# A statically ordered attention and mixer kernel: shorter latencies in the order's model, and stage settings chosen anew for them

## The chip, the cores and the metric

One core of a Trainium2 chip. The metric is the device time of one execution in microseconds. Every run of a kernel was timed on the same chip as runs of the kernel before, in alternating rounds; medians are given with the lowest and highest run. The clock quoted is the mean TensorE clock that was granted in a run, as a share of full speed.

## The reference

The input `x` has 2048 rows of 512 values. A gate per row mixes two branches: attention with 32 heads of width 16, and a mixer with two layers. Everything is bfloat16.

```python
def reference(A_x, A_wqkv, A_wo, B_x, B_w1, B_w2, B_w3, B_w4, gate_w):
    def _A_ref(x, wqkv, wo):
        ...                                   # q, k, v: 32 heads of 16
        scores = jnp.einsum("bhqd,bhkd->bhqk", q, k) * (Dh ** -0.5)
        p = _softmax(scores, axis=-1)
        o = jnp.einsum("bhqk,bhkd->bhqd", p, v)
        return (...)(o, 0, 2, 1, 3).reshape(B, S, D) @ wo
    def _B_ref(x, w1, w2, w3, w4):
        h = _gelu(_layernorm(x, axis=-1) @ w1)
        ...                                   # four column groups shifted by 1 or 2 rows
        hs = jnp.concatenate([g0, g1, g2, g3], axis=-1) @ w2
        x1 = x + hs
        h2 = _gelu(_layernorm(x1, axis=-1) @ w3) @ w4
        return x1 + h2
    g = _sigmoid((x * gate_w).sum(-1, keepdims=True))
    return g * a + (1 - g) * b                # a, b: the two branches
```

The scores make 2048 tiles of 128 keys by 512 queries, and all of them have to be exponentiated. ScalarE does it with its own function, in pairs of tiles; VectorE does it for about 28% of the tiles by arithmetic on the bits of the number, with the help of shifted copies that VectorE or GpSimd makes. At the end of each round but the last (32 rounds, each of four heads and 512 queries) the sums are copied out of PSUM.

## The kernel before

The order of instructions on each engine is not written by hand. While the program is built, the kernel runs a small event model of the five engines, picks what an engine does next whenever it is free, and emits instructions in the order of the model's times. On the chip each engine works through its list strictly in that order, and semaphores hold it where a result is missing. So the model's numbers (`hold`, how long an engine is taken, and `lat`, how much later the result counts as seen) never hold anything up on the chip; they only decide the order.

```python
class Job:
    def __init__(self, eng, hold, lat, deps, fn, prio=5, acq=(), frees=(), at=0, name="", port=False): ...

class Sim:
    def emit(self, t, fn):
        if fn is not None:
            self.n += 1
            self.order.append((t, self.n, fn))

    def try_engine(self, e):
        ...                                    # the ready job of the best priority is j
        j.start = self.t
        self.emit(self.t, self.in_port_order(e, j.fn) if j.port else j.fn)
        self.t_free[e] = self.t + j.hold
        ...
        self.push(self.t + j.hold + j.lat, lambda: self.finish_job(j))   # only now do dependents become ready
```

The helpers give each engine its latency. Line 321 holds the settings by stage: 32 score tiles are a stage, and a stage may overrule any of 24 numbers of the picking rule (how far ahead scores run, when a shift goes to GpSimd, how urgent the end of one of the 32 rounds, each of four heads and 512 queries, is, and so on). They come from a search outside the kernel.

```python
    def dve(hold, deps, fn, **kw):
        return sim.add(Job("DVE", hold, 280.0, deps, fn, **kw))
    def act(hold, deps, fn, **kw):
        return sim.add(Job("ACT", hold, 160.0, deps, fn, **kw))
    def gp(hold, deps, fn, **kw):
        return sim.add(Job("POOL", hold, 250.0, deps, fn, port=True, **kw))
    def dma(lat, deps, fn, hold=450.0, **kw):
        return sim.add(Job("SP", hold, lat - hold, deps, fn, **kw))
```

At the end of each round but the last (32 rounds, each of four heads and 512 queries) the sums are copied out of PSUM, and the softmax denominators in them go through two transfers: first to a small buffer `den` in DRAM, then back, spread over 128 partitions, to `pk`. VectorE then forms reciprocals. The model takes 2.0 us for each transfer:

```python
    def finish_round(r):
        ...
        e = dve(PSUM_NS, round_ops[r], lambda: nc.vector.tensor_copy(out=ab.slot[:], in_=acc[:]), acq=[ab], prio=0)  # L1033
        d0 = dma(2000.0, [e], lambda: nc.sync.dma_start(out=db.slot[:], in_=ab.slot[0:P:32, :]), prio=1, acq=[db],
                 frees=[ab])                                                                                       # L1036
        d1 = dma(2000.0, [d0], lambda: nc.sync.dma_start(
            out=kb.slot[:], in_=db.slot[:].rearrange("j (b e) -> (j b) e", e=16)), prio=1, acq=[kb], frees=[db])   # L1038
        r1 = dve(160, [d1], lambda: nc.vector.reciprocal(out=kb.slot[:], in_=kb.slot[:]), prio=0)                  # L1040
        r2 = dve(90, [r1] + jg[1], ...)          # times the gate
        d2 = dma(2000.0, [r2], ...)              # pk to DRAM, then four broadcasts d3 to bcs
        n = gp(1250, d3, lambda: nc.gpsimd.tensor_tensor(out=ob.slot[:], in0=ab.slot[:], in1=bb.slot[:], op=ALU.mult),
               acq=[ob], frees=[ab, bb], prio=0)                                                                   # L1050
```

The second place is the normalised input of the mixer, `xn`: VectorE writes 32 tiles into two buffers in turn, and each goes to DRAM by a transfer before its buffer is free again.

```python
        for t in range(4 * c, 4 * c + 4):
            xb = Buf("xn", 1)
            g = dve(323, [m], lambda t=t, xb=xb: nc.vector.tensor_scalar(out=xb.slot[:], in0=x_sb[:, t, :], ...),
                    prio=0.35, acq=[xb], port=True)                                                                # L695
            ds.append(dma(2200.0, [g], lambda t=t, xb=xb: nc.sync.dma_start(
                out=xn_dram[which, t * P:(t + 1) * P, :], in_=xb.slot[:]), frees=[xb]))
```

The softmax here doesn't subtract the row's maximum and nothing guards it: scores larger than these inputs give would overflow.

## Time and profile before

| | before |
|---|---|
| median of the first 3 runs (lowest to highest) | 772.55 us (772.16 to 772.81) |
| span of the profiled execution, granted clock | 770.4 us, 1.000 |
| ScalarE waiting before its pairs (L922) | 16.8 us |
| VectorE waiting for score tiles in the ring (L948) | 23.6 us in 62 pieces |
| VectorE waiting for a transfer | 0.3 us (0.2 us of it in the one piece that the list below shows) |

Three engines are over 94% busy, so a microsecond in which ScalarE, VectorE or TensorE stands still between 20 and 755 us can be a loss of time. The prediction below shows the main groups and stretches. One line of the list of waits of the kernel before is needed besides. A line says who waited at which line for whom, then the total in us, how often, and the longest:

```profile
DVE pk L1040 <- DMA pk<-den: 0.2, 1, 0.2
```

The reader is to see that VectorE's reciprocals, which depend on a transfer, cost practically no waiting in this kernel.

### The profile page before, as it was taken

How to read it: one execution, taken by the hardware profiler on the slowest of the kernel's cores; microseconds unless marked ns; L12 is line 12 of the kernel's file. 1: busy time of each engine (PE TensorE's matmuls, PEld its weight loads, DVE VectorE, ACT ScalarE, POOL GpSimd, SP SyncE). 2: the span in 40 equal slices, each digit the busy share in tenths (PEclk: the TensorE clock that was granted, in tenths of full speed). 3: DMA queues.
4: the chain of work that ended last, by engine and by line, in shares of the span. 5: the costliest groups of instructions: out<-in, count | busy, mean ns of one | idle time of the engine just before them, and what ended most of it. 6: DMA issues, size and time to landing. Idle time of an engine off the chain costs nothing.

```text
span 770.4 us, 23725 instructions
## 1 busy us (share of the span) xinstructions
PE 758.7 (98%) x9588; PEld 227.8 (30%) x9588; DVE 725.2 (94%) x1575; ACT 739.7 (96%) x767; POOL 335.2 (44%) x332
## 2 busy tenths in 40 slices
PE   9999999999999999999999999999999999999997
PEld 5333322223222222233232224222233222223222
DVE  6999999999999999998989998999999889999996
ACT  6899999999999999999989999999999999999995
POOL 2345533443344444344345553344454454454531
PEclk9999999999999999999999999999999999999999
DMA  9402133122001221141001001001100000000001
GB/s 192 142 3 35 54 98 88 47 72 89 6 19 34 61 72 46 48 125 50 17 18 33 23 20 47 23 27 27 41 19 19 23 19 22 27 20 20 13 18 38
DMA packets 67093, 34.60 MB, mean 45 GB/s; under 512 B 46748, under 2 KB 62380, under 8 KB 66984
## 3 DMA queue, kind: packets, MB, share of 16 engines
q1 hardware_dynamic: 66040, 32.56, 16.3%
q8 instruction: 75, 1.23, 0.6%
q10 hardware_dynamic: 944, 0.52, 0.2%
q14 instruction: 34, 0.28, 0.1%
HBM read 17.40 MB, written 6.81 MB: 31 GB/s over the span
## 4 chain that ended last, share of the span: by engine, by line
PE 71%; ACT 22%; DVE 4%; issue 3%; ACTq 0%; DVEq 0%
PE acc L1017 26%; PE psA L842 23%; PE ring L532 20%; ACT PA L922 16%; DVE PD L948 2%; ACT hT L766 2%; ACT hB L766 2%; DVE PD L984 1%; ACT hT L735 1%; ACT L922 1%; PE ring L842 1%; PE ring L510 0%; ACT L766 0%; PE ring L1295 0%; DVE hB L765 0%
## 5 line engine op out<-in xcount | busy, mean ns | idle before, releaser
L922 ACT ACTIVATE PA<-psA 128x1024 bf16<-128x1024 f32 x742 | 689.8, 1052 | 16.8 <-PE acc L1017 7.7
L986 POOL TENSOR_SCALAR PD<-PD 128x1024 uint16<-128x1024 uint16 x270 | 281.8, 1048 | 384.7 <-DVE PD L984 215.8
L948 DVE TENSOR_SCALAR PD<-ring 128x512 uint16<-128x512 f32 x565 | 372.9, 680 | 25.9 <-PE ring L842 23.6
L1017 PE MATMUL acc<-PD,V 128*17 128x512 bf16 x2260 | 307.3, 381 | 1.0 <-DVE accsb L1033 0.8
L842 PE MATMUL psA<-q,kT 32*128 32x512 bf16 x1483 | 285.8, 384 | 5.3 <-ACT PA L922 4.4
L1017 PE MATMUL acc<-PA,V 128*17 128x512 bf16 x1483 | 277.6, 381 | 0.0
L984 DVE TENSOR_SCALAR PD<-PD 128x1024 uint16<-128x1024 uint16 x579 | 226.2, 429 | 1.5 <-PE acc L1017 0.8
L842 PE MATMUL ring<-q,kT 32*128 32x512 bf16 x565 | 190.7, 384 | 0.0
L842 PEld LDWEIGHTS <-kT 32*128 32x128 bf16 x2048 | 76.8, 91 | 311.0 <-issue 309.0
L1017 PEld LDWEIGHTS <-V 128*17 128x17 bf16 x3743 | 74.9, 88 | 129.1 <-issue 107.0
L532 PE MATMUL ring<-xnT,w 128*32 128x512 bf16 x1152 | 89.0, 382 | 0.0
L532 PE MATMUL ring<-w,hT 128*32 128x512 bf16 x704 | 58.5, 383 | 0.1
L532 PEld LDWEIGHTS <-w 128*32 128x32 bf16 x1920 | 45.2, 95 | 43.9 <-issue 30.3
L1050 POOL TENSOR_TENSOR oT<-accsb,bcs 128x512 bf16<-128x512 f32 x31 | 39.5, 1275 | 24.7 <-DVE PD L984 19.4
L532 PE MATMUL ring<-w,w 128*32 128x256 bf16 (+1 forms) x768 | 41.1, 311 | 0.0
L532 PE MATMUL ring<-w,hB 128*32 128x512 bf16 x448 | 36.0, 383 | 0.0
L1033 DVE COPY accsb<-acc 128x512 f32<-128x512 f32 x31 | 21.1, 681 | 1.1 <-PE acc L1017 1.0
L675 DVE BATCH_NORM_STATS2 st<-x_sb 128x6 f32<-128x512 bf16 x32 | 21.5, 678 | 0.0
L532 PE MATMUL ring<-w,wq 128*32 128x512 bf16 x256 | 21.2, 383 | 0.2 <-ACT w L561 0.2
L532 PEld LDWEIGHTS <-hT 128*32 128x32 bf16 x704 | 14.8, 95 | 20.3 <-issue 15.5
L765 DVE CAST hT<-ring 128x512 bf16<-128x512 f32 x28 | 18.8, 680 | 1.1 <-PE ring L532 0.9
L765 DVE CAST hB<-ring 128x512 bf16<-128x512 f32 x28 | 19.0, 682 | 0.9 <-PE ring L532 0.7
(93 smaller groups left out, 263.5 us busy)
## 6 DMA issues: line engine op xcount, KB each, us to landing
bcs<-rr SPq DMA_DIRECT2D x124, 64.0 KB
xn_dram<-xn SPq DMA_DIRECT2D x32, 128.0 KB
w<-in_B_w_dram SPq DMA_DIRECT2D x5, 512.0 KB
oD<-oT SPq DMA_DIRECT2D x124, 16.0 KB
w<-in_B_w_dram SPq DMA_DIRECT2D x4, 448.0 KB
out_dram<-ot SPq DMA_DIRECT2D x14, 128.0 KB
x_sb<-in_A_x_dram SPq DMA_DIRECT2D x3, 512.0 KB
w<-in_A_wqkv_dram SPq DMA_DIRECT2D x2, 256.0 KB
```

The source lines that it names most:

```text
L532: units.append([Op("col", j, lambda j=j, lf=lf, rf=rf, n0=n0, n1=n1, st=st, sp=sp: nc.tensor.matmul(get()[32 * j:32 * j + 32, n0:n1], lhsT ...
L675: a = dve(600, deps, lambda: nc.vector.bn_stats(out=sb.slot[:], in_=x_sb[:, t, :]), prio=6, at=at, acq=[sb])
L765: pre.append(evac(g, PSUM_NS, lambda ps, m=m: nc.vector.tensor_copy(out=h2()[:, m, :], in_=ps[:])))
L766: ge = act(93 + 427 * FT + 2600, pre, lambda: nc.scalar.activation(out=h2(), in_=h2(), func=ACT.Gelu_apprx_tanh), prio=0)
L842: o = Op("row", i, lambda: nc.tensor.matmul(dst(), lhsT=kT[G][32 * i:32 * i + 32, kt * P:(kt + 1) * P], rhs=qbuf[G, c].slot[32 * i:32 * i ...
L922: job = act(hold, ops, lambda: nc.scalar.activation(out=pb.slot[:, 0:n], in_=buf.slot[:, 0:n], func=ACT.Exp, scale=0.25), acq=[pb], frees= ...
L948: nc.vector.tensor_scalar(out=pr["buf"].slot[:, h * 512:(h + 1) * 512], in0=buf.slot[:], scalar1=BITS_MUL, scalar2=BITS_ADD, op0=ALU.mult, ...
L984: return nc.vector.tensor_scalar(out=d[k][:, 0:w], in0=d[0][:, 0:w], scalar1=float(SHIFT * k), scalar2=None, op0=ALU.add)
L986: return nc.gpsimd.tensor_scalar(out=d[k][:, 0:w], in0=d[0 if both else 2][:, 0:w], scalar1=1.0, scalar2=float(SHIFT * (k if both else 1)) ...
L1017: o = Op("col", i, lambda: nc.tensor.matmul(acc[32 * i:32 * i + DH + 1, :], lhsT=lhs(), rhs=rhs(), start=st, stop=True, tile_position=(0, ...
L1033: e = dve(PSUM_NS, round_ops[r], lambda: nc.vector.tensor_copy(out=ab.slot[:], in_=acc[:]), acq=[ab], prio=0)
L1050: n = gp(1250, d3, lambda: nc.gpsimd.tensor_tensor(out=ob.slot[:], in0=ab.slot[:], in1=bb.slot[:], op=ALU.mult), acq=[ob], frees=[ab, bb], ...
```

## The change

The model's latencies for VectorE and GpSimd results are cut until the model's time from the start of an instruction to that of its dependant is close to the measured one (the prediction below works it out: 0.03 us above it), and the settings by stage are chosen anew under the shorter latencies. The idea: a model without slack can place dependants right behind their results, and packs the order tighter.

```diff
-    STAGES = {0: {'AHEAD': 6, 'EARLY': 13, 'DVE_ALONE': 150, 'S_PRIO': 0.368}, 1: {'AHEAD': 8, 'S_PRIO': 0.415}, ... }   # cut
+    STAGES = {0: {'GP2': 0.1, 'DUE_SH': -20}, 1: {'SL': (165, 180), 'PRESS': 30}, ... }                                 # cut
     def dve(hold, deps, fn, **kw):
-        return sim.add(Job("DVE", hold, 280.0, deps, fn, **kw))
+        return sim.add(Job("DVE", hold, 150.0, deps, fn, **kw))
     def gp(hold, deps, fn, **kw):
-        return sim.add(Job("POOL", hold, 250.0, deps, fn, port=True, **kw))
+        return sim.add(Job("POOL", hold, 110.0, deps, fn, port=True, **kw))
     def evac(g, hold, fn, prio=2, eng="DVE", **kw):
-        job = Job(eng, hold, 280.0, ...)
+        job = Job(eng, hold, 150.0, ...)
```

More of the change, by code (lines that the diff above doesn't have):

```diff
@@ L320 @@
     SEG = 32
-    STAGES = {0: {'AHEAD': 6, 'EARLY': 13, 'DVE_ALONE': 150, 'S_PRIO': 0.368}, 1: {'AHEAD': 8, 'S_PRIO': 0.415}, 2: {'ROT': 3, 'URG': 3, 'MAXU': 9, 'PD_LOW': 3}, 3: {'PA_LOW': 3, 'DVE_WAIT': 4}, 4: {'SL': (25, 60), 'URG': 2, 'DVE_STOP_L': 9, 'DUE_SH': 40}, 5: {'SL': (25, 60), 'URG': 2, 'DVE_STOP_L': 9, 'DUE_SH': 40}, 6: {'S_PRIO': 0.234}, 7: {'PRESS': 17, 'DVE_WAIT': 5}, 8: {'PV_FULL': 0.776, 'AHEAD': 7, 'PD_LOW': 0}, 9: {'PV_FULL': 0.877, 'ROT': 2, 'AHEAD': 6, 'PA_LOW': 0}, 10: {'PV_FULL': 0.794, 'PA_LOW': 0, 'SL': (165, 60), 'DVE_ALONE': 2}, 11: {'SL': (85, 100), 'EARLY': 62}, 12: {'EARLY': 124, 'PV_IDLE': 0.433, 'DVE_STOP_L': 11, 'SL': (25, 40)}, 13: {'GP3': 0.6, 'DVE_ALONE': 150}, 14: {'ROT': 3, 'GP3': 0.9, 'URG_L': 16, 'AHEAD2': 12}, 15: {'P1_PRIO': 0.309, 'DVE_STOP_L': 5, 'AT_SH': 60, 'DVE_STOP': 5}, 16: {'DVE_WAIT': 2, 'AHEAD2': 10}, 17: {'ROT': 1, 'AT_SH': 10, 'GP3': 0.8, 'DVE_ALONE': 2}, 18: {'P1_PRIO': 0.403, 'GP2': 0.2}, 19: {'PRESS': 10}, 20: {'URG': 7, 'AT_SH': 60, 'GP2': 0.2}, 21: {'IDLE_NS': 352, 'DVE_ALONE': 300}, 22: {'S_PRIO': 0.257}, 23: {'PRESS': 52, 'AT_SH': 60}, 24: {'PA_LOW': 3, 'PRESS': 23, 'GP3': 0.8}, 25: {'PV_IDLE': 0.414, 'AT_SH': 10}, 26: {'DUE_SH': 8, 'PD_LOW': 1, 'GP2': 0.2, 'GP3': 0.9}, 28: {'AHEAD2': 10, 'EARLY': 142}, 29: {'AHEAD': 8, 'S_PRIO': 0.388, 'GP3': 0.9, 'ROT': 1}, 30: {'PV_IDLE': 0.372, 'DUE_SH': -40, 'S_PRIO': 0.412, 'PA_LOW': 2}, 31: {'IDLE_NS': 311, 'GP3': 0.9, 'P1_PRIO': 0.22}, 32: {'DUE_SH': 40, 'DVE_STOP': 5}, 33: {'DVE_STOP_L': 7, 'SL': (205, 60)}, 34: {'P1_PRIO': 0.326, 'PD_LOW': 0, 'PV_IDLE': 0.37, 'GP2': 0.35}, 36: {'PD_LOW': 1, 'DVE_STOP': 7}, 37: {'URG': 4, 'IDLE_NS': 589}, 38: {'ROT': 2}, 39: {'EARLY': 155, 'PA_LOW': 3}, 40: {'DUE_SH': -20, 'PRESS': 8}, 41: {'P1_PRIO': 0.584, 'PA_LOW': 3, 'MAXU': 10}, 42: {'AHEAD2': 8, 'PRESS': 58, 'DVE_ALONE': 0}, 43: {'PD_LOW': 0, 'DVE_WAIT': 2, 'P1_PRIO': 0.216, 'PV_FULL': 1}, 44: {'MAXU': 7, 'ROT': 1}, 45: {'PRESS': 10, 'SL': (65, 80)}, 46: {'DVE_WAIT': 6, 'AT_SH': 120, 'PD_LOW': 0}, 47: {'DUE_SH': 80, 'P1_PRIO': 0.59, 'DVE_ALONE': 150, 'AHEAD2': 6}, 48: {'URG': 8, 'AT_SH': 120}, 49: {'PD_LOW': 3, 'ROT': 3, 'DVE_WAIT': 6, 'AT_SH': 120}, 50: {'DVE_WAIT': 1, 'SL': (5, 60), 'GP2': 0.35, 'DVE_STOP_L': 11}, 51: {'PA_LOW': 3, 'URG_L': 18}, 52: {'ROT': 2, 'PD_LOW': 1, 'PRESS': 35}, 53: {'URG_L': 16, 'IDLE_NS': 245, 'PRESS': 19}, 54: {'PD_LOW': 3}, 56: {'MAXU': 10, 'GP2': 0.1}, 57: {'URG': 2}, 58: {'ROT': 3, 'DVE_WAIT': 5}, 59: {'ROT': 1}, 60: {'GP2': 0.2, 'PV_FULL': 0.879, 'SL': (85, 100)}, 61: {'GP3': 0.6, 'GP2': 0.35, 'PV_FULL': 0.985}, 62: {'GP3': 0.6, 'GP2': 0.35, 'PV_FULL': 0.985}}
@@ new lines @@
+    STAGES = {0: {'GP2': 0.1, 'DUE_SH': -20}, 1: {'SL': (165, 180), 'PRESS': 30}, 2: {'ROT': 2, 'AT_SH': 120, 'PD_LOW': 0}, 3: {'PA_LOW': 1}, 4: {'S_PRIO': 0.598, 'GP3': 0.9, 'MAXU': 7, 'DVE_STOP': 9}, 5: {'IDLE_NS': 854, 'DVE_STOP_L': 9, 'SL': (85, 100)}, 6: {'SL': (125, 60), 'AHEAD2': 7}, 7: {'S_PRIO': 0.268, 'DVE_STOP': 8, 'PV_FULL': 0.864, 'URG': 2}, 8: {'ROT': 3, 'DVE_STOP': 7}, 9: {'PA_LOW': 1}, 10: {'GP2': 0.2, 'SL': (165, 60), 'AHEAD': 6}, 11: {'PV_FULL': 0.7, 'AHEAD2': 12}, 12: {'SL': (5, 20), 'DVE_STOP': 7, 'PA_LOW': 3, 'GP2': 0.35}, 13: {'AHEAD': 10, 'GP3': 0.8}, 14: {'P1_PRIO': 0.411, 'DVE_WAIT': 1, 'SL': (65, 60), 'PV_FULL': 1}, 15: {'DUE_SH': 8, 'DVE_STOP': 9, 'PA_LOW': 2, 'PD_LOW': 0}, 16: {'EARLY': 159, 'PV_IDLE': 0.105}, 17: {'PV_IDLE': 0.545, 'EARLY': 9}, 18: {'AHEAD2': 10, 'GP3': 0.8, 'AT_SH': 10, 'DUE_SH': -20}, 19: {'PA_LOW': 1, 'URG': 4}, 20: {'PRESS': 50, 'PD_LOW': 2, 'SL': (165, 180), 'DVE_STOP': 7}, 21: {'URG': 2, 'SL': (125, 60)}, 22: {'S_PRIO': 0.506, 'ROT': 1}, 23: {'GP3': 0.6, 'DUE_SH': 8}, 24: {'AT_SH': 30, 'GP2': 0.1, 'MAXU': 4, 'PV_IDLE': 0.35}, 25: {'GP2': 0.2}, 26: {'PRESS': 50, 'DVE_ALONE': 500, 'AT_SH': 60, 'SL': (205, 60)}, 27: {'SL': (25, 40)}, 28: {'GP2': 0.1, 'URG': 4}, 29: {'URG': 3, 'MAXU': 8, 'AT_SH': 120}, 30: {'MAXU': 11, 'PA_LOW': 0, 'DVE_ALONE': 500}, 31: {'PA_LOW': 1, 'MAXU': 7, 'GP3': 0.8}, 32: {'SL': (85, 60), 'GP2': 0.35, 'ROT': 2, 'DUE_SH': -8}, 33: {'S_PRIO': 0.295, 'SL': (165, 60), 'AHEAD': 8, 'DUE_SH': -40}, 34: {'DVE_ALONE': 500, 'DVE_STOP_L': 5, 'AHEAD2': 11, 'DVE_STOP': 5}, 35: {'PV_FULL': 0.684, 'URG_L': 19, 'PA_LOW': 2, 'PD_LOW': 0}, 36: {'DVE_ALONE': 0, 'AT_SH': 60}, 37: {'ROT': 2, 'PD_LOW': 0, 'DVE_WAIT': 2}, 38: {'EARLY': 138}, 39: {'URG': 3, 'DUE_SH': -8, 'DVE_ALONE': 2, 'PA_LOW': 3}, 40: {'PA_LOW': 3}, 41: {'DVE_STOP': 4, 'GP3': 0.8}, 42: {'ROT': 3}, 43: {'DUE_SH': 20, 'DVE_STOP_L': 10, 'DVE_STOP': 4, 'GP2': 0.35}, 44: {'URG': 4, 'ROT': 2}, 46: {'MAXU': 7, 'URG_L': 18, 'PV_IDLE': 0.292, 'GP2': 0.35}, 47: {'AT_SH': 60, 'PA_LOW': 3, 'EARLY': 115, 'IDLE_NS': 616}, 48: {'S_PRIO': 0.557, 'GP2': 0.1, 'DVE_STOP': 8, 'PV_FULL': 0.713}, 51: {'SL': (25, 60), 'AHEAD': 11, 'PV_IDLE': 0.46, 'S_PRIO': 0.395}, 53: {'AHEAD2': 7, 'GP3': 0.6}, 54: {'ROT': 3}, 55: {'DVE_STOP': 5, 'EARLY': 142, 'PRESS': 53}, 56: {'ROT': 2, 'EARLY': 154, 'PRESS': 37, 'IDLE_NS': 353}, 57: {'ROT': 1}, 58: {'DVE_STOP': 3, 'IDLE_NS': 321, 'DVE_ALONE': 300}, 59: {'ROT': 1, 'GP3': 0.9}, 60: {'PRESS': 14, 'GP2': 0.1, 'DVE_STOP': 4, 'URG_L': 15}, 61: {'PA_LOW': 1, 'DVE_ALONE': 300, 'P1_PRIO': 0.512, 'DVE_STOP': 9}, 62: {'SL': (5, 20)}, 64: {'DVE_ALONE': 2, 'SL': (25, 40)}}
@@ L541, in evac @@
     def evac(g, hold, fn, prio=2, eng="DVE", **kw):
-        job = Job(eng, hold, 280.0, [g.units[-1][-1]] if not COL else g.units[-1], lambda: fn(g.buf.slot), prio=prio,
+        job = Job(eng, hold, 150.0, [g.units[-1][-1]] if not COL else g.units[-1], lambda: fn(g.buf.slot), prio=prio,
                   frees=[g.buf] + kw.pop("frees", []), **kw)
```

## The prediction

> **What bounds the kernel now.** I read the granted clock first (1.000 on the one core, so nothing is throttled), then the page's busy shares, the groups by shape, the waits, and a table of stretches. The page's first part:
>
> ```profile
> span 770.4 us, 23725 instructions
> PE 758.7 (98%) x9588; PEld 227.8 (30%) x9588; DVE 725.2 (94%) x1575; ACT 739.7 (96%) x767; POOL 335.2 (44%) x332
> ```
>
> Three engines are nearly full at once. The work on them is fixed by how the 2048 score tiles are split: ScalarE exponentiates two tiles per instruction (L922), VectorE makes a tile by arithmetic on bits (L948) and two or three shifted copies per pair (L984), and TensorE then multiplies one matrix with V per ScalarE tile but four per VectorE tile. The groups by shape:
>
> ```profile
> L922 ACT ACTIVATE PA<-psA 128x1024 bf16<-128x1024 f32 x741 | 689.3, 1053 | 16.8 <-PE acc L1017 7.7 <-PE psA L842 4.9 <-PE ring L842 2.5
> L948 DVE TENSOR_SCALAR PD<-ring 128x512 uint16<-128x512 f32 x565 | 372.9, 680 | 25.9 <-PE ring L842 23.6 <-PE acc L1017 0.5 <-PE psA L842 0.4
> L1017 PE MATMUL acc<-PD,V 128*17 128x512 bf16 x2260 | 307.3, 381 | 1.0 <-DVE accsb L1033 0.8
> L986 POOL TENSOR_SCALAR PD<-PD 128x1024 uint16<-128x1024 uint16 x270 | 281.8, 1048 | 384.7 <-DVE PD L984 215.8 <-PE ring L842 43.7 <-PE acc L1017 39.2
> ```
>
> To see: ScalarE waits only 16.8 us before its 741 pairs; VectorE waits 23.6 us, in 62 pieces by the list of waits, for score tiles in the PSUM ring; TensorE waits for almost nobody; GpSimd has half its time free. The stretches (columns: PE, PEld, DVE, ACT, POOL busy):
>
> ```profile
> 0.00:20.00 20.00, 18.56 (x285) 10.21 (x286) 12.86 (x30) 12.66 (x17) 5.97 (x16) 1.00 0.99 188
> 20.00:380.00 360.00, 357.15 (x4485) 106.38 (x4481) 353.00 (x800) 354.73 (x371) 153.12 (x150) 1.00 0.22 59
> 380.00:420.00 40.00, 39.96 (x535) 11.44 (x530) 36.50 (x76) 36.35 (x40) 17.01 (x17) 1.00 0.08 24
> 420.00:755.00 335.00, 331.76 (x4175) 96.28 (x4171) 314.20 (x654) 328.33 (x334) 157.80 (x149) 1.00 0.09 24
> 755.00:771.00 16.00, 11.23 (x126) 3.45 (x124) 8.69 (x21) 7.65 (x10) 1.32 (x2) 0.98 0.12 38
> ```
>
> To see: between 20 and 755 us ScalarE is idle for 735 - (354.73 + 36.35 + 328.33) = 15.6 us. The other half of its idle time is start-up (7.3 us before 20) and tail (8.3 us after 755). An order of instructions can win back mainly the 15.6 us.
>
> **How tight the latencies are.** The kernel holds an event model of the five engines; run while the program is built, it decides the order of every engine's instructions, with the settings by stage. On the chip only semaphores hold things. The change concerns how long the model thinks a result takes to be seen after an instruction's slot. The timeline at a round's end, and at a shift that waits for its own tile:
>
> ```profile
> 436.05 0.67 DVE L1033 COPY accsb<-acc 128x512 f32<-128x512 f32 x1
> ...
> 436.77 0.39 PE L1017 MATMUL acc<-PD,V 128*17 128x512 bf16 x2 [0.23 <-DVE accsb L1033]
> ```
> ```profile
> 333.23 0.68 DVE L948 TENSOR_SCALAR PD<-ring 128x512 uint16<-128x512 f32 x1
> 333.95 0.85 DVE L984 TENSOR_SCALAR PD<-PD 128x1024 uint16<-128x1024 uint16 x1
> ```
> ```profile
> 433.82 1.05 POOL L986 TENSOR_SCALAR PD<-PD 128x1024 uint16<-128x1024 uint16 x1 [1.11 <-PE acc L1017]
> ...
> 434.92 0.39 PE L1017 MATMUL acc<-PD,V 128*17 128x512 bf16 x2
> ```
>
> To see: start to dependent start is 0.72 us for each of the two VectorE cases and 1.10 us for GpSimd. The model has a slot of 0.598 or 0.600 us plus 0.28, so 0.88 us, for the first two, and 1.018 + 0.25 = 1.27 us for GpSimd. So the model before is late by some 0.16 us everywhere. With the new constants it says 0.75 and 1.13 us: still 0.03 us above the chip.
>
> **What the Trainium skill says.** "Perfetto Trace Analysis", section "Per-instruction lifecycle", says that a Vector or Scalar instruction's reported end is the write's acknowledgement with the semaphore push, and that the propagation comes after it, unreported. The trace agrees: 0.05 us lie between the copy's end and the matmul. The same page, "Identifying the Most-Contended Engine", warns that matmul busy share does not measure TensorE's headroom; so I do not take the 98% for a limit by itself. "TensorEngine Tiling (Array Packing)", "Key Properties", says that changing the tiling mode drains TensorE. The chain of work shows it: a score turn of two or three matmuls takes 0.32 us though one 512-column step takes 0.22 (a 12-matmul column turn takes 0.76 us, an 8-matmul one 0.54; the difference is one step). "TensorE: Matmul & The Clock Gate", "Architectural detail", says that Vector and Scalar queues are strictly first in, first out; so a wrongly placed instruction holds all behind it. This trace does not contradict that: the stalls above have work queued behind them.
>
> **The change part by part.** I built both programs and compared their instructions; no time was taken from that. The dataflow is the same, and the counts hardly move:
> - ScalarE pairs: 741 plus one half become 740 whole. The half took 0.65 us, of which some 0.49 is slot; a pair costs 0.92 (0.904 to 0.92 start to start). Minus 1.4 us of ScalarE.
> - VectorE tiles 565 to 568, at 0.60 us: plus 1.8 us; shifts 576 + 3 halves to 575, at 0.34 us: minus 1.1 us (halves taken as 0.25 us). Plus 0.7 us of VectorE. GpSimd shifts 270 to 277, at 1.02 us: plus 7 us, beside 384.7 us of waiting, so free.
> - TensorE: score turns 742 to 739, column steps 1963 to 1960. Three turns at 0.32 + 0.11 us (the second is what an 8-matmul column turn takes above two steps) and three steps at 0.22: minus 1.9 us. Fillers 112 to 108, inside that.
> - Depth: the median number of matmuls between a score matmul and the product that uses it goes from 54 to 55 by ScalarE, and from 54 to 52 by VectorE. At 9588/742, some 13 matmuls a turn, results wait four turns, about 4 us. A 0.13 us shorter latency is small against that, and most of it is hidden.
> - Where it is not hidden: ring slots. The model sees a slot free 0.13 us sooner. Between a read's end and the next write the trace shows a median of 0.57 us. If each of the 62 ring waits shrinks by 0.13, VectorE gains 8.1 us; it makes 28% of the tiles, and I let a third reach the end: minus 2.7 us. At 31 round ends the next round's products are admitted 0.13 us sooner, 4.0 us; other column work mostly fills that, so a third: minus 1.3 us.
> - The new settings themselves: a search under a truer model should close part of the 15.6 us. I choose a fifth: minus 3 us. This is the softest term.
> - Against it: with 0.03 us of slack a late result stalls TensorE in order. I put plus 1.5 us. The tail has a whole last pair for a half: plus 0.4 us.
> - Less work on the shared bound: minus 1 us.
> The sum: -2.7 - 1.3 - 3 + 1.5 + 0.4 - 1 = -6.1 us, so 766.5 us.
>
> **Rivals.** First, TensorE stalls take the slack's place: the order is packed to 0.03 us, so every jitter of a VectorE or GpSimd result shows as a wait of products (L1017) for L948, L984 or L986. It would cost 3 to 10 us and bring 775 or more. For it: all engines are above 94%, so a stall is not absorbed. Against it: the depth of four turns, and constants that still lie above the measured latencies. Second, nothing happens: 0.13 us is lost in queues of 4 us, counts are the same, and the span stays at 770 to 773. For it: waits for products of a full PA pool (7.7 us of the 16.8) have nothing to do with these latencies. Third, the new settings pack much better, and most of the 15.6 us goes: 758 to 760. Against it: VectorE and TensorE would have to hold the same pace, and they have only 45 and 12 us unbusy, start and tail included.
>
> **Range and chances.** Faster by over 2% means below 757.1 us: 15.4 us, as good as all of ScalarE's idle time between start-up and tail. I give it 0.07. Slower by over 2% means above 788.0, which would double that idle time; 0.03. The range 759.5 to 774 leaves room for the third rival at one end and a mild first at the other.
>
> **What would show it.** Right: ScalarE's waits at L922 fall from 16.8 to about 11 us; VectorE's ring waits fall from 23.6 us towards 16; TensorE still waits for nearly nobody; durations of single instructions are unchanged. Wrong: products (L1017) waiting for VectorE or GpSimd by several us (first rival); waits unchanged in sum and only moved to other stages (second); ScalarE idle between 20 and 755 us below 6 us (third). The prediction would also be wrong if start-up or tail, which I hold fixed within 1 us, moved by several.

## The result, and the profile after

The changed kernel took 773.71 us (772.89 to 775.82, 4 runs), the kernel before on the same chip 772.36 us. The ratio is 1.0022, with a 95% interval of 1.0001 to 1.0042. So nothing was gained; the forecast was a gain of 6 us. The profiled execution spans 771.7 us at a mean clock of 0.998.

The first part of the page of the changed kernel, and its groups by shape (busy us, mean ns of one, then idle time before them and what ended it):

```profile
span 771.7 us, 23735 instructions
PE 757.2 (98%) x9593; PEld 225.2 (29%) x9593; DVE 727.1 (94%) x1574; ACT 740.6 (96%) x765; POOL 341.4 (44%) x339
```
```profile
L922 ACT ACTIVATE PA<-psA 128x1024 bf16<-128x1024 f32 x740 | 690.8, 1045 | 17.8 <-PE acc L1017 5.9 <-PE psA L842 5.6 <-PE ring L842 5.0
L948 DVE TENSOR_SCALAR PD<-ring 128x512 uint16<-128x512 f32 x568 | 375.3, 683 | 18.5 <-PE ring L842 15.9 <-PE acc L1017 0.3 <-PE psA L842 0.2
L1017 PE MATMUL acc<-PD,V 128*17 128x512 bf16 x2272 | 301.6, 382 | 2.6 <-DVE PD L984 1.8 <-POOL PD L986 0.5 <-DVE accsb L1033 0.2
...
L695 DVE TENSOR_SCALAR xn<-x_sb,rs,nm 128x512 bf16<-128x512 bf16 x32 | 11.7, 407 | 2.1 <-DMA xn_dram<-xn 2.1
L1040 DVE RECIPROCAL pk<-pk 128x16 f32<-128x16 f32 x31 | 7.6, 245 | 5.0 <-DMA pk<-den 5.0
```

The ring waits did fall as forecast, from 23.6 to 15.9 us, and single instructions last as long as before. But ScalarE waits 17.8 us instead of less, and two lines have waits of a new kind: VectorE stands 5.0 us at reciprocals and 2.1 us at `xn` tiles, for transfers. The list of waits says in how many pieces:

```profile
DVE pk L1040 <- DMA pk<-den: 5.0, 5, 1.9
...
DVE xn L695 <- DMA xn_dram<-xn: 2.1, 3, 0.8
```

The longest is at 182.6 us. The timeline there (start, duration, engine, line, operation; in brackets the idle time before and what ended it):

```profile
182.64 0.25 DVE L1040 RECIPROCAL pk<-pk 128x16 f32<-128x16 f32 x1 [1.85 <-DMA pk<-den]
182.81 0.36 DVE L984 TENSOR_SCALAR PD<-PD 128x1024 uint16<-128x1024 uint16 x1
...
183.23 0.39 PE L1017 MATMUL acc<-PD,V 128*17 128x512 bf16 x2 [1.22 <-DVE PD L984]
...
184.49 1.02 ACT L922 ACTIVATE PA<-psA 128x1024 bf16<-128x1024 f32 x1 [1.12 <-PE psA L842]
...
185.16 0.61 PE L842 MATMUL psA<-q,kT 32*128 32x512 bf16 x2
```

These lines show the mechanism. VectorE has reached the reciprocal and stands 1.85 us, because its operand is still in transit. The shift L984 is next in its list and has its data, but must wait behind. TensorE needs that shift for a product and stands 1.22 us; ScalarE needs scores that TensorE would have made in that time and stands 1.12 us. One late transfer of 8 KB has stopped all three full engines. The last line shows a second effect: a matmul of 512 columns takes 0.61 us instead of the 0.39 of the matmul at 183.23 us.

The stretches around it (us, busy time of PE, PEld, DVE, ACT, POOL, granted clock, DMA share, GB/s):

```profile
176.00:180.00 4.00, 3.84 (x49) 1.12 (x48) 3.05 (x6) 4.00 (x6) 1.55 (x2) 1.00 0.77 291
180.00:185.00 5.00, 3.59 (x34) 0.95 (x33) 2.95 (x8) 3.88 (x5) 1.04 (x1) 1.00 0.04 5
185.00:189.00 4.00, 4.00 (x27) 0.64 (x25) 2.98 (x7) 2.72 (x4) 1.04 (x1) 0.57 0.20 66
```

The denominators' first transfer was issued at 176.5 us, while four weight loads of 448 KB filled 77% of the transfer engines, and the second could only be issued 4.42 us later; the usual distance of the two issues in this trace is 1.72 us. The packet records of the trace say where that time went: the last of its four packets moved at 180.0 us, 3.5 us after the issue (usually 1.35), when the last packet of the weight loads had just ended (179.8 us). After the stall the clock of TensorE was halved for 3.4 us (0.57 in the last row), in which ScalarE worked 2.72 of 4 us.

**How far the chip lags behind its plan.** The kernel's own model can serve as a ruler. It has a planned start for every ScalarE pair; the trace has the actual start. Their difference, the drift, shows where the chip falls behind the plan. The plan's end is a number of the program's build, not a chip time; it is used only together with the drift. Over all kernels, the span is the plan's end plus the final drift plus about 8.4 us (7.5 to 8.5; mostly the tail after the model's last matmul).

| kernel | plan's end | final drift | profiled span |
|---|---|---|---|
| before | 764.6 | -2.6 | 770.4 |
| changed | 759.4 | +3.8 | 771.7 |

The new settings are worth 5.2 us in the plan. The kernel before was 2.6 us ahead of its plan at the end, since its latencies were pessimistic; the changed kernel fell 3.8 us behind. Its drift is nearly flat but for a rise of 2.9 us (from -0.7 to +2.2) between 183 and 197 us and steps of 0.75 us at 365.8, 0.73 at 636.0 and 0.66 us at 728.5. Three of these four come right after VectorE's waits for denominators: 1.85 us at 182.6, 1.25 at 632.6 and 1.14 us at 726.9. The step at 365.8 us comes 12 us after the nearest such wait, 0.63 us for an `xn` buffer at 353.8, so its cause is less plain.

### The profile page after: what moved, and what is told of

Its sections match the earlier page's. It is cut to its first block, busy times and chain, and to the rows that moved or that the text cites. A ratio compares the mean times of both kernels' runs of the same rounds, so it can differ in the third digit from the quotient of the medians.

```text
span 771.7 us, 23735 instructions
## 1 busy us (share of the span) xinstructions
PE 757.2 (98%) x9593; PEld 225.2 (29%) x9593; DVE 727.1 (94%) x1574; ACT 740.6 (96%) x765; POOL 341.4 (44%) x339
## 4 chain that ended last, share of the span: by engine, by line
PE 70%; DVE 17%; ACT 5%; DMA 4%; issue 2%; SPq 1%; POOL 0%; POOLq 0%; DVEq 0%; ACTq 0%
PE acc L1017 25%; PE psA L842 22%; PE ring L532 21%; DVE PD L948 7%; DVE PD L984 5%; ACT PA L922 3%; DMA pk<-den 1%; DMA xn_dram<-xn 1%; DMA den<-accsb 1%; ACT hT L735 1%; ACT hT L766 1%; DVE accsb L1033 1%; DVE hT L765 1%; DVE st L675 1%; PE ring L842 1%
## 5 line engine op out<-in xcount | busy, mean ns | idle before, releaser
L922 ACT ACTIVATE PA<-psA 128x1024 bf16<-128x1024 f32 x740 | 690.8, 1045 | 17.8 <-PE acc L1017 5.9
L986 POOL TENSOR_SCALAR PD<-PD 128x1024 uint16<-128x1024 uint16 x277 | 288.1, 1044 | 377.8 <-DVE PD L984 219.5
L948 DVE TENSOR_SCALAR PD<-ring 128x512 uint16<-128x512 f32 x568 | 375.3, 683 | 18.5 <-PE ring L842 15.9
L1017 PE MATMUL acc<-PD,V 128*17 128x512 bf16 x2272 | 301.6, 382 | 2.6 <-DVE PD L984 1.8
L1017 PE MATMUL acc<-PA,V 128*17 128x512 bf16 x1480 | 268.2, 382 | 0.0
L984 DVE TENSOR_SCALAR PD<-PD 128x1024 uint16<-128x1024 uint16 x575 | 224.7, 431 | 4.8 <-PE acc L1017 1.5
L842 PE MATMUL ring<-q,kT 32*128 32x512 bf16 x568 | 193.5, 386 | 0.5 <-DVE PD L948 0.5
L842 PEld LDWEIGHTS <-kT 32*128 32x128 bf16 x2048 | 75.2, 91 | 310.1 <-issue 309.2
L532 PE MATMUL ring<-w,hT 128*32 128x512 bf16 x704 | 56.6, 384 | 0.0
L1050 POOL TENSOR_TENSOR oT<-accsb,bcs 128x512 bf16<-128x512 f32 x31 | 40.3, 1300 | 25.1 <-DVE PD L984 13.5
```

The costliest lines, as they stand in the source:

```text
L532: units.append([Op("col", j, lambda j=j, lf=lf, rf=rf, n0=n0, n1=n1, st=st, sp=sp: nc.tensor.matmul(get()[32 * j:32 * j + 32, n0:n1], lhsT ...
L842: o = Op("row", i, lambda: nc.tensor.matmul(dst(), lhsT=kT[G][32 * i:32 * i + 32, kt * P:(kt + 1) * P], rhs=qbuf[G, c].slot[32 * i:32 * i ...
L922: job = act(hold, ops, lambda: nc.scalar.activation(out=pb.slot[:, 0:n], in_=buf.slot[:, 0:n], func=ACT.Exp, scale=0.25), acq=[pb], frees= ...
L948: nc.vector.tensor_scalar(out=pr["buf"].slot[:, h * 512:(h + 1) * 512], in0=buf.slot[:], scalar1=BITS_MUL, scalar2=BITS_ADD, op0=ALU.mult, ...
L984: return nc.vector.tensor_scalar(out=d[k][:, 0:w], in0=d[0][:, 0:w], scalar1=float(SHIFT * k), scalar2=None, op0=ALU.add)
L986: return nc.gpsimd.tensor_scalar(out=d[k][:, 0:w], in0=d[0 if both else 2][:, 0:w], scalar1=1.0, scalar2=float(SHIFT * (k if both else 1)) ...
```

## The experiments

The theory that the experiments test: the tighter order is worth some 4 to 5 us, and late transfers at which VectorE stands in order (reciprocals, `xn` tiles), with the lost clock after them, take it back. The rivals: the new order is no better in itself (the settings or the lost slack of engine results hold it back), or the loss is only the clock. Where an expected text has letters for theories, the numbers beside each say what it would give. All kernels were run beside the kernel before, five rounds unless noted; its medians lay between 772.2 and 772.6. Every kernel gave the right result but e9, e10 and e11, which are wrong. Executions over 1.5% slower than the fastest of the same kernel are left out of the means.

### First attempt: emit the waiting instructions later

**e1_rc.** The reciprocal and all that follows it in a round is emitted 1.5 us later than planned, so that the transfer has time.

```diff
-        self.emit(self.t, ...)
+        self.emit(self.t + j.shift, ...)
         ...
+        SH = 1500.0 if r < NR - 3 else 0.0
-        r1 = dve(160, [d1], ..., prio=0)
+        r1 = dve(160, [d1], ..., prio=0, shift=SH)      # the same for r2, d2, d3, n, d4
```

> The changed kernel with the reciprocal of the denominators and all that follows from it (its scaling, the transfers behind it, the GpSimd product) placed 1.5 us later in every engine's order; nothing else of the order moves. Theory A (the gain of the truer latencies is given back where VectorE, strictly in order, stands before a transfer that lands later than the order assumed, five times for 5.0 us in the trace of the changed kernel, once with the TensorE clock halved behind it): the waits of L1040 for its transfer fall from 5.0 to under 1 us, the clock stays at 1.000, and the time falls by 2 to 4 us, to 769.5 to 771.5. Theory B (the order is packed too tight for the chip everywhere, small lateness of VectorE and GpSimd results): the time stays within 1 us of 773.7, since the waits only show in other places.

Measured: 779.13 us (778.69 to 780.46), ratio 1.0092. The waits at reciprocals fell from 5.0 to 1.2 us, but the kernel is slower. The transfers moved too in their queue, and GpSimd now stands longer at the product of a round (in this kernel L1051; in the changed kernel it was 10.1 us in 3 pieces):

```profile
POOL oT L1051 <- DMA bcs<-rr: 13.4, 6, 6.1
```

The longest of these, 6.1 us, ends at 108.6 us, and between 108.5 and 115 us the drift rises by 4.8 us. So the edit took one wait away and made a larger one; it does not decide.

**e2_xn.** The same for the third and fourth `xn` tile of each group and for what follows them, 1.0 us later (`shift=1000` in `normalise` and one later VectorE job).

> The changed kernel with the third and fourth normalised tile of each chunk, their transfers and the transposes behind them placed 1.0 us later in the order; nothing else moves. Theory A: the waits of L695 for the transfer out of its buffer (three, 2.1 us in the trace of the changed kernel) go, and the time falls by 0.5 to 1.5 us, to 772.2 to 773.2. Theory B: unchanged, 773 to 774.5.

Measured: 775.03 us (772.39 to 777.62, 6 runs), ratio 1.0045; the profiled execution spans 770.5 us. The steps of the drift at 52 and 366 us are gone in it, but the runs scatter by 5 us with their clock (1.000 to 0.992). Inconclusive.

**e3_both** has both edits, **e4_before_both** is the control: the same two edits in the kernel before, which has nothing to gain from them.

> Both shifts in the changed kernel. Theory A: VectorE waits for transfers nearly nowhere (7.1 us before, under 1 us here), the clock stays at 1.000 in all runs, and the time is 768.5 to 770.5: the 3.8 us by which the chip ran behind the plan in four steps are gone, and it is below the kernel before by 0.2 to 0.5 percent. Theory B: within 1 us of 773.7.

> Control: the same two shifts in the kernel before, which had two such waits of 0.3 us in all. Theory A: within 0.7 us of 772.4. A rival theory C (moving these instructions later helps any order, for example by taking small VectorE work out of the way of the score tiles) expects 2 to 4 us less, as in the changed kernel.

Measured: 779.40 us (ratio 1.0093) and 780.98 us (1.0114). The control lost 8.8 us, and e3 5.7 us against the changed kernel that it was made from. Moving instructions in a packed order costs by itself, whatever it cures; these four kernels decide nothing about the theory.

### Second attempt: move VectorE and GpSimd alone

If every transfer is emitted 1.5 us later, no engine's own order changes; a VectorE job emitted 1.5 us later too keeps its place against transfers but moves back on VectorE.

```diff
-        self.emit(self.t, ...)
+        self.emit(self.t + (1500.0 if e == "SP" else j.shift), ...)
         ...
+        SH, SN = (1500.0, 2500.0) if r < NR - 3 else (0.0, 0.0)     # SH: reciprocal, r2;  SN: product on GpSimd
```

**e5_rc_alone** does it for reciprocals, **e6_both_alone** for `xn` too, **e7_before_both_alone** is e6 in the kernel before.

> As the first experiment, but with the order of TensorE, ScalarE and the transfer queue left exactly as in the changed kernel (the first one also moved transfers against each other, and GpSimd then stood 5 us before one at 113 us): in VectorE's order the reciprocal and its scaling stand 1.5 us later, in GpSimd's the product 2.5 us later. Theory A (late transfers in front of VectorE cost the gain): waits of the reciprocal under 1 us in all instead of 5.0, the three late steps at 185 to 189, 636 and 728 us gone, clock 1.000, time 769.5 to 771.5, that is 2 to 4 us under the changed kernel. Theory B (packed too tight everywhere): within 1 us of 773.7. Theory D (the transfer queue itself, strictly in order too, passes the delay on to the product and the output): 774 or more, with new waits at L1050.

> The same and in addition the third and fourth normalised tile of each chunk 1.5 us later in VectorE's order alone. Theory A: under 1 us of waits of VectorE for transfers, 768.5 to 770.5, below the kernel before. Theory B: within 1 us of 773.7. Theory D: 774 or more.

> Control, the same edits in the kernel before, whose VectorE waits 0.3 us for transfers. Theory A: within 0.7 us of 772.2. Theory C (later small work helps any order): 2 us less or more. Theory D: 774 or more.

Measured: 791.58 us (787.83 to 794.12; ratio 1.0246), 788.30 us (1.0208) and 788.23 us (1.0207). Again the control loses as much: 16 us, as against 15 for e6 and 18 for e5, counted from the changed kernel. The waits of e5:

```profile
POOL oT L1050 <- DVE PD L984: 35.2, 15, 5.5
PE acc L1017 <- POOL PD L986: 5.5, 10, 1.1
```

The product of the round (1.3 us on GpSimd) now comes later in GpSimd's list, the shifts behind it too, and TensorE stands 5.5 us for GpSimd's shifts where it stood 0.5 us. The waits that the edit was to take away did not all go either (3.2 us at one reciprocal, 6.6 us at `xn` tiles). The time is in the range that theory D gave, with new waits at L1050 as it said, but the trace puts them on VectorE's shifts and not on the transfer queue. What follows for the main question: an instruction in this order cannot be moved for free, so the wait itself has to be taken away with the order untouched.

### Make the wait in the kernel before

**e8_before_early.** In the kernel before, which has no such waits, the reciprocal is emitted 1.0 us earlier (`shift=SH`, `SH = -1000.0`, on `r1` alone).

> The suspected cost put into the kernel before: its reciprocals stand 1.0 us earlier in VectorE's order (the scaling and all other engines stay). Theory A: 15 or more of 29 reciprocals now wait for their transfer, 5 to 15 us in all, and the time rises by 2 to 8 us, to 774 to 780, with the clock under 1.000 in some runs. Theory B: the kernel before has slack of 0.13 us in every result, so 772 to 773.

Measured: 775.82 us (774.71 to 776.43), ratio 1.0043 (1.0031 to 1.0056). Its waits:

```profile
DVE pk L1040 <- DMA pk<-den: 7.0, 9, 1.6
```

Nine of the reciprocals wait, where 15 or more were expected. The plan is unchanged (764.6), the drift went from -2.6 to +1.6 us, the span from 770.4 to 774.6 us: in this profile, that of the slowest of the five runs, 7.0 us of waits at reciprocals go with a loss of 4.2 us. Over all five runs the loss is 3.3 us (the ratio), about half of the waits. This is the disputed cost made in the other kernel; since an instruction was moved for it, a part may be the cost of the move. It says what such waits cost, not yet that they are what the changed kernel lacks.

### Take the waits away, order untouched

**e9_no_pk_wait.** The reciprocal reads a constant tile, and the transfer lands in a tile that nobody reads; every engine's list stays as it is.

```diff
-            out=kb.slot[:], in_=db.slot[:].rearrange("j (b e) -> (j b) e", e=16)), ...)
+            out=rdl[:],     in_=db.slot[:].rearrange("j (b e) -> (j b) e", e=16)), ...)
-        r1 = dve(160, [d1], lambda: nc.vector.reciprocal(out=kb.slot[:], in_=kb.slot[:]), prio=0)
+        r1 = dve(160, [d1], lambda: nc.vector.reciprocal(out=kb.slot[:], in_=mhalf[:]), prio=0)
```

> The changed kernel with every engine's order exactly as it is, but the reciprocal reads a constant tile and the transfer of the denominators, still issued, lands in a tile that nobody waits for. So the wait is taken away and nothing else; the result is wrong on purpose. Theory A (late transfers in front of VectorE cost the gain; in the reverse experiment 7.0 us of such waits cost 3.6 us): 5.0 us of waits go, so 2 to 4 us less than the changed kernel, 770 to 771.7, and no clock loss at 185 us. Theory B (packed too tight everywhere): within 0.7 us of 773.7.

Measured: 769.55 and 769.76 us at a clock of 1.000; 772.84, 772.87 and 773.79 at 0.995 to 0.996; and one run of 3573.78 us, which was the profiled one: TensorE was busy 3567 of 3572 us in it, and a matmul took 1.56 us on average where it takes 0.38. That run is unexplained and set aside (one run of the kernel before took 2197.03 us, so it is not this edit's). Ratio 0.9994 (0.9976 to 1.0011). Two things follow: the reciprocals' waits alone are worth some 3 us at full clock (769.7, two runs, against the changed kernel's 772.6, the mean of its four runs at a clock of 1.000), and runs with a lower clock were longer by as much again.

**e10_no_waits** also takes the `xn` wait away: the transfer to DRAM reads a constant tile (`in_=woL[:]`), so the buffer is free at once. **e11_before_no_waits** is the control, the same in the kernel before.

> The same, and the normalised tiles' transfers read another tile, so that VectorE never waits for a buffer to be sent (result wrong on purpose). Theory A: VectorE waits for no transfer at all, the chip keeps to the plan to within 1 us at the end instead of running 3.8 us late, clock 1.000 in all runs, 768.5 to 770.3, faster than the kernel before by 0.25 to 0.5 percent. Theory B: within 0.7 us of 773.7.

> Control, the same edits in the kernel before, which has 0.3 us of such waits. Theory A: 771.7 to 772.5, unchanged. If it falls by 2 us too, the waits are not what set the two kernels apart.

Measured: e10 768.41 us (767.37 to 770.10), ratio 0.9952 (0.9939 to 0.9964); e11 772.43 us (771.63 to 772.64), ratio 1.0001 (0.9989 to 1.0013). This is the decisive pair. The same edit, without moving an instruction, is worth nothing in the kernel before and about 5 us in the changed one (ratio 1.0022 to 0.9952).

The profiled run of e10 shows that the clock is a matter of its own. There is no stall of TensorE over 0.34 us in the 9 us before it, and yet (columns as above):

```profile
212.00:216.00 4.00, 3.80 (x30) 0.96 (x29) 3.05 (x7) 3.70 (x4) 2.09 (x2) 0.60 0.08 21
216.00:220.00 4.00, 4.00 (x34) 0.68 (x34) 2.34 (x5) 2.41 (x3) 1.04 (x1) 0.55 0.00 0
```

### One half of the change alone

**e12_new_latencies_old_settings** (3 rounds): the kernel before with 150, 150 and 110 in place of 280, 280 and 250. **e17_new_settings_old_latencies** (3 rounds): the changed kernel with the old latencies.

> One part of the change alone: the new latencies with the settings by stage of before. The kernel's own plan then ends 18.5 us later than that of before, since each set of settings was searched for its own latencies. Theory A holds that the chip keeps to a plan but for late transfers: 788 to 795. A rival theory E (the latencies alone bring a gain and the new settings lose it) expects under 772.

> The other part of the change alone: the new settings by stage with the old latencies. The plan made at build ends at 792.4 us, 27.8 us later than that of before. Where the chip keeps to the plan (spans were 8.4 us above the plan's end in the kernels before and after, once the drift is taken off), and gets back some 2.5 us as the kernel before did: a span of 796 to 801, a time of 798 to 803. A theory that the settings are better for the chip whatever the latencies expects under 773.

Measured: 794.24 us (793.76 to 795.18; ratio 1.0286) and 800.84 us (799.25 to 801.68; 1.0362). Either half alone loses 22 or 28 us. The plans said so already (783.1 and 792.4, with drifts of +1.4 and -0.9 us). The settings by stage fit one set of latencies and do badly with the other; the change's two halves cannot be priced separately. A new search under the old latencies was not tried, so it is not shown that the plan's 5.2 us need the shorter latencies.

Both halves have the waits of the new kind: VectorE stands 3.2 us at reciprocals and 2.5 us at `xn` tiles in e12, and 3.9 and 1.4 us in e17, which has the old latencies. So it is not the cut of the latencies by itself that brings them. Of the four orders that were made here, the kernel before is the one that is nearly free of them.

### A version that keeps the result right

**e13_fix.** The denominators go in one transfer from the copied sums to `pk`, without the stop in DRAM, and the third and fourth `xn` tile of each group use two output buffers that lie idle at that time. In the model a job without an instruction stands for the second transfer, so the orders of all engines but the transfer queue's stay as they are.

```diff
-        d0 = dma(2000.0, [e], lambda: nc.sync.dma_start(out=db.slot[:], in_=ab.slot[0:P:32, :]), prio=1, acq=[db], frees=[ab])
-        d1 = dma(2000.0, [d0], lambda: nc.sync.dma_start(
-            out=kb.slot[:], in_=db.slot[:].rearrange("j (b e) -> (j b) e", e=16)), prio=1, acq=[kb], frees=[db])
+        d0 = dma(2000.0, [e], lambda: nc.sync.dma_start(
+            out=kb.slot[:], in_=ab.slot[0:P:32, :].rearrange("j (b e) -> j b e", e=16)), prio=1, acq=[db, kb], frees=[ab])
+        d1 = dma(2000.0, [d0], None, prio=1, frees=[db])
-                out=xb.slot[:], in0=x_sb[:, t, :], ...        # and in_=xb.slot[:] of its transfer
+                out=(xot[t % 2] if t % 4 > 1 else xb.slot)[:], in0=x_sb[:, t, :], ...
```

> The changed kernel, result right: the denominators go from the copied accumulator straight into the packed tile, one transfer instead of two over a scratch in memory, while VectorE's reciprocal keeps its place in the order; and every third and fourth normalised tile uses a buffer that is free at that time. All orders but the transfer queue's are the same. Theory A: no waits of VectorE for these transfers (7.1 us in the changed kernel, under 0.5 us here), and as in the wrong-result pair 767.4 to 770.5, median about 768.5, faster than the kernel before by about 0.5 percent. Theory B: 773 to 774.5. Theory F (the direct transfer is slow, since it reads four partitions): new waits at the reciprocal, 772 or more.

Measured: 768.09 us (767.47 to 769.47), ratio 0.9946 (0.9934 to 0.9958), right result. It beats both kernels, by 0.5% and 0.7%; the interval is clear of 1. From its page and its groups:

```profile
span 766.3 us, 23658 instructions
```
```profile
L922 ACT ACTIVATE PA<-psA 128x1024 bf16<-128x1024 f32 x740 | 689.4, 1047 | 12.9 <-PE acc L1017 5.9 <-PE ring L842 3.2 <-PE psA L842 2.5
L948 DVE TENSOR_SCALAR PD<-ring 128x512 uint16<-128x512 f32 x568 | 374.4, 680 | 19.3 <-PE ring L842 15.8 <-PE psA L842 0.7 <-PE acc L1017 0.3
L1040 DVE RECIPROCAL pk<-pk 128x16 f32<-128x16 f32 x31 | 7.4, 239 | 0.0
```

VectorE no longer stands for a transfer at all, TensorE no longer for VectorE or GpSimd at its products (2.6 us before), and ScalarE's waits are 12.9 us instead of 17.8. The same weight loads are in flight at 176 us, and nothing comes of it:

```profile
176.00:180.00 4.00, 3.60 (x46) 1.02 (x45) 3.05 (x7) 4.00 (x6) 1.80 (x2) 1.00 0.88 328
180.00:185.00 5.00, 5.00 (x56) 1.41 (x52) 4.31 (x11) 5.00 (x6) 1.26 (x2) 1.00 0.12 36
185.00:189.00 4.00, 4.00 (x48) 1.12 (x44) 4.00 (x10) 4.00 (x6) 1.29 (x2) 1.00 0.08 28
```

**e14_fix_warm** adds 17 matmuls with zeros in the planned stretch of 210 to 214.5 us, where e10 had lost its clock.

> The same with 17 matmuls of zeros more in the stretch behind the first gelu (planned 210 to 214.5 us), where TensorE has some 35 matmuls in 4 us and waits for ScalarE. If the drop of the clock in e10 at 213 us came from that sparse stretch: clock 1.000 in all runs, and all within 767 to 768.3, 0.5 to 1 us under the median of e13. If the drop comes from elsewhere: the same scatter as e13. If these matmuls are not hidden: up to 1 us more.

Measured: 768.26 us (767.19 to 768.40), ratio 0.9943 (0.9930 to 0.9956): not to be told from e13. One run of e13 had a lower clock (0.997, 769.47 us), none of e14 was below 0.999; with one such run there is nothing to tell. Inconclusive.

**e15_before_fix** is e13's edit in the kernel before, **e16_after_again** the changed kernel again, in the same rounds. (In e16's text every transfer is emitted 1.5 us later and nothing else, which changes no engine's order: the built program is that of the changed kernel.)

> Control: the same two edits in the kernel before, which had no such waits. Theory A: 771.6 to 772.6, the same as the kernel before. If it too falls by 2 us or more, the shorter transfers help for another reason.

> The changed kernel once more, on the same chip as the three others (its program is the same instruction for instruction). 772.9 to 776, scattering with the clock: runs at 1.000 under 773.2, runs at 0.998 or lower above 773.5.

Measured: e15 772.67 us (771.70 to 772.90), ratio 1.0001 (0.9989 to 1.0013); e16 772.98 us (771.39 to 775.68, 6 runs), ratio 1.0012 (0.9996 to 1.0028). e16's profile answers the rival that the loss is only the clock. Its clock stays at full speed from 4.9 us to 768 us, and yet its span is 771.7 us and its final drift +3.8 us, as in the first profile of this program, and the waits are there:

```profile
DVE pk L1040 <- DMA pk<-den: 4.4, 5, 1.7
...
DVE xn L695 <- DMA xn_dram<-xn: 3.6, 4, 1.4
```

The four kernels of these rounds are a table of two by two:

| ratio to the kernel before | with the two transfers as they were | with e13's edit | what the edit is worth |
|---|---|---|---|
| old latencies and settings | 1 | 1.0001 | nothing |
| new latencies and settings | 1.0012 | 0.9946 | -5.1 us |
| what the change is worth | +0.9 us | -4.2 us | |

(In us at 772.4 us: 0.0066 x 772.4 = 5.1; 0.0055 x 772.4 = 4.2; 0.0012 x 772.4 = 0.9.) The profiled spans say the same: 770.4, 769.9, 771.7 and 766.3 us, so -3.6 us for the change without late transfers and +5.4 us for the late transfers in the changed kernel, against +0.5 us in the kernel before; -3.6 + 5.4 - 0.5 = +1.3 us, the difference of the two profiled spans.

## Why the prediction was wrong

**The bound, the counts and the durations were right.** ScalarE's pairs, VectorE's tiles, GpSimd's shifts and TensorE's turns came out as counted (740, 568, 277), and single instructions kept their durations. The tail stayed within 1 us (ScalarE idle for 8.25 us after 755 us, before 8.35). The start did not: in the first 20 us ScalarE is busy 14.53 us instead of 12.66, 1.9 us more, where the prediction held the start fixed within 1 us. From 20 to 755 us ScalarE's idle time went from 15.6 to 17.6 us where it was to fall by some 6 us.

**The ring waits were right.** They fell to 15.9 us, against a forecast of 16.

**The first rival, as it was put, is refuted.** TensorE waits only 2.6 us at products, of which 1.8 us are for VectorE's shifts, and 1.22 of those lie behind the late transfer at 182 us. In e13, with the same order and the same slack of 0.03 us, TensorE waits at products for nobody. So results of VectorE and GpSimd were not late by themselves. The rival's shape was right, with the wrong late party: a stall passed on in order, since all engines are full.

**The step that failed is the line "Against it".** It put 1.5 us for late results, and looked for them among the results whose latency the change touches. The cost was 5.1 us (5.4 in the profiles), and the late party were transfers, whose constants the change did not touch: VectorE stood 5.0 us at reciprocals and 2.1 us at `xn` tiles, and TensorE and ScalarE behind it. The prediction doesn't mention transfers. It could take the two waits for them in the kernel before (0.3 us) as harmless, and never asked how near the others were. The model gives the denominators 4.0 us for two transfers; VectorE came to its reciprocals 4.3 us after the copy's end in the median (4.4 us in the kernel before), and in the worst case the reciprocal could start only 6.1 us after it. So the closer packing took hardly any of that room, 0.1 us; what the new order changed is which transfers meet other traffic.

In the worst case it was the first transfer, to DRAM, that was late, amid heavy traffic: 4.42 instead of 1.72 us between the two issues at 77% DMA share, 2.7 us more. "DMA: Bandwidth & Descriptors" of the Trainium skill, in "Anatomy of one DMA" (of transfers that GpSimd issues), calls the roughly 2 us of a transfer mostly the wait until the last byte is confirmed in the target memory, with HBM the heaviest, and in "Latency and other measured facts" gives HBM access 0.2 us on average and 2 us at high load. The trace agrees that load makes a transfer longer, but not on where the time goes: 3.5 of the 4.42 us had passed when the last packet had moved (1.35 of 1.72 usually), so 2.2 of the 2.7 us were lost before the data had moved and 0.5 us after. In e13 the one transfer straight into the on-chip tile was issued at a share of 0.88 at the same place; its data too moved late, 2.9 us after the issue (usually 1.6), but VectorE came only 4.2 us after it.

**The gain was mis-sized too.** Without that term the prediction's sum is -6.1 - 1.5 = -7.6 us. With the late transfers gone, the change is worth -4.2 us (-3.6 in the profiles). The plan itself shortened by 5.2 us, and part of that the kernel before had already without any change: its latencies were too long (by 0.16 us in the prediction's three cases) only on paper, and on the chip it ran ahead of its plan, by 3.1 us in e15. The changed kernel with e13's edit runs ahead by 1.5 us. So 1.6 us of the plan's 5.2 were slack that the chip had never spent; 5.2 - 1.6 = 3.6. The prediction's terms for ring waits (-2.7) and round ends (-1.3) probably counted such slack as a gain; no run separates them from the term for the settings (-3).

**ScalarE's waits** were to fall to about 11 us. They rose to 17.8, and fell to 12.9 when the late transfers were gone.

**The second rival, nothing happens,** named the right span (770 to 773 us; 771.7 measured) for the wrong reason: the new order does reach the end, and something else takes it back. That the measured time lies inside the range given (759.5 to 774) is luck too: its upper end was kept for the first rival, which did not happen.

**The clock** has a smaller part in the loss. At a clock of 1.000 the changed kernel's four runs have a mean of 772.6 us and e13's four 767.9, still 4.7 us apart, so most of the loss is the waits and not the clock; e16's profile says the same. At the wait near 183 us the drift rises by 2.9 us in the profile with the halved clock and by 1.4 us in e16's without. Single runs of one kernel with a lower clock were 3 to 4 us longer (e9: 769.7 against 772.8 to 773.8). "TensorE: Matmul & The Clock Gate", "What's actually happening", says that the clock halves after at least one idle window of about 3.4 us. The trace fits the length of such a window (the clock stays halved for 3.4 us here and for 6.8 us, twice that, in e10), but shows no idle one: the longest idle time of TensorE before it was 1.22 us here and 0.34 us in e10. The same page's section on psum-queue depth-cycling has such a case, with short idle times between groups of matmuls.

**What stays open.** Why the old order escaped late transfers is shown in part. The second transfers issued at 629.0 and 723.4 us, with little traffic, held VectorE for 1.25 and 1.14 us in the changed kernel, each with 3.6 us between issue and reciprocal, while no reciprocal of the kernel before started more than 3.3 us after its issue, and it had slow first transfers too (3.86 us at 415 us, without a wait, since VectorE was at other work). The packet records name what held these two: 120 of the 128 packets had moved 1.4 us after the issue, and the last eight only when one packet of 16 KB in the queue that the profile calls `instruction` had ended, 1.0 us later. In the first case, from 630.4 to 631.7 us (queue, packets, MB, share of the 16 engines):

```profile
q8 instruction: 1, 0.02, 4.9%
q1 hardware_dynamic: 9, 0.00, 1.1%
```

e16's profile has the same at both places, so it belongs to the order and is no accident of one run. Each of the two kernels has 72 such packets between 20 and 760 us; in the kernel before, one of them held up a second transfer (at 556 us), when VectorE was at other work. This is read from the traces; no run tests it. The model knows of no such packets, so the old order may simply have been lucky, unless its search looked at times on the chip. Whether warm matmuls keep the clock is open as well.

## What to carry to other kernels

A new order made with truer latencies for one kind of result helps only as far as every other latency that an in-order engine can stand on has room for its worst case, and here that was the transfers, not the semaphores. Where a full engine stands for a transfer, shorten the transfer's path (one hop instead of two, a buffer more) and leave the order alone; moving instructions in a packed order cost 5 to 18 us in six of the eight kernels in which it was tried, two controls among them, counted from the kernel that was edited (e2 and e8 lost 1 and 3 us). And lay the plan over the trace: its drift shows in steps where the time went, and how much of the planned gain the chip already had.

## What the Trainium skill lacked or had wrong

- "DMA: Bandwidth & Descriptors" gives a fixed cost of about 2.0 us as nearly constant, from transfers that GpSimd issued. These small transfers were issued from SyncE, and what matters for an in-order plan is the spread: between the issue of the first (to DRAM) and that of the second 1.72 us in the median, 4.42 us at worst. Of the direct one to on-chip memory the trace has no landing, only that its last packet had moved 1.6 us after the issue in the median and 2.9 us at worst. The page says that load changes the fixed cost; no page has such a spread.
- "TensorE: Matmul & The Clock Gate" names an idle window of about 3.4 us as what halves the clock, and short idle times between groups as a second way, without a number. In e10 it was halved from about 212.8 to 219.6 us with no idle time over 0.34 us in the 9 us before, after a stretch of 38 matmuls in 4 us; the changed kernel kept its full clock at the same place in a stretch of 27 in 4 us (212 to 216 us). So the number of matmuls does not tell either, and no page says what does.
- No page says how a build-time plan should budget a transfer's latency against a semaphore's: 0.03 us of slack was enough for VectorE and GpSimd results, while 4.0 us for two transfers was exceeded by up to 2.1 us.
- No page gives what a packet of the instruction queue costs another transfer: one of 16 KB, on its way for 1.0 us, came before the last eight of 128 packets of a transfer of 8 KB, which then ended 2.7 us after its issue, usually 1.3. It would belong to "Runtime: NRT & Kernel Launch", section "Instruction fetch mechanics".
